# GpSimd takes up two of its transferred sums earlier, VectorE one sum one place earlier, and x and results are issued three slots later

## The chip, the cores and the metric

The kernel runs on one core of a Trainium2 chip. The metric is the device time of one execution in microseconds (us). Below, PE is TensorE, DVE is VectorE, ACT is ScalarE, POOL is GpSimd and SP is SyncE, as in the profile; a transfer is a DMA.

## The reference

The input is x, 8 sequences of 4096 tokens of 192 numbers. First comes a causal convolution over 7 tokens; its 7 weights come from a softmax and are shared by the 24 numbers of one of 8 heads. Then comes a two-layer network with an exact GELU between the products.

```
w = softmax(weight, axis=-1)                       # 8 heads x 7 taps
x_unf = x_pad[:, idx, :].reshape(B, S, K, H, 24)   # 6 zeros ahead of each sequence
x1 = einsum('hk,bskhg->bshg', w, x_unf)            # (8, 4096, 192)
h = x1.reshape(32768, 192) @ w_in                  # (192, 2048)
out = gelu(h) @ w_out                              # (2048, 192), float32
```

## The kernel before

**Tiles and stages.** The 32768 tokens are two halves of 16384; partitions 0 to 63 carry numbers of the first half and 64 to 127 of the second. A tile is 512 tokens of each half (the first six tiles have 256). For tile n, SP loads x in four transfers into one of three `xin` buffers (`load`, L570); DVE turns it so that the 192 numbers lie along the partitions (L747, letter `t` of `ORDER`) and computes the seven taps, two instructions for each tap (L775, letter `c`), into `xc`. In stage n, PE multiplies `xc` by `w_in` in 16 slots (`mm1`, L991); ACT applies the GELU to each slot's result (L896) and leaves `gT`. Between the slots of stage n, PE runs the second product of tile n-1. Its result is turned by DVE into `osb`, and SP stores that in four transfers (`store`, L590).

**The tiles with sums.** For tiles 6 to 33 the second product is written out by hand. Thirteen of them, the even tiles m = 8, 10, ..., 32 (`ST` in the code), use a scheme with fewer multiplications (`mm2_s`, L1129): it runs in stage m+1, and takes as operands four sums of blocks of `gT`, kept in `sst`. The sums are called S1, S3, Dn and S4. S1 and S3 are made in four pieces each (0 to 3), Dn and S4 in two. Dn adds to S1, and S4 adds to Dn. A piece of S1 or S3 needs the GELUs of four slots of stage m: piece 0 needs the first 3 or 4, piece 1 the first 7 or 8, piece 2 the first 11 or 12, piece 3 the first 15 or 16. The other tiles use the plain form (`mm2_t`, L1069).

**Who makes the sums.** Five pieces are made by transfers that POOL issues (`BY_DMA`): S3 pieces 0, 1, 2 and S1 pieces 0, 1. Each takes two transfers of 256 KB: a copy of the first operand from `gT` to `sst` (L494; POOL waits for the GELUs), and an adding transfer of the second operand (L497; POOL waits until the copy has landed). The other seven pieces are additions on DVE (L487, letters `1`, `3`, `d`, `4` of `ORDER` for S1, S3, Dn, S4). A piece 0 of Dn on DVE waits for the adding transfers of S1 pieces 0 and 1.

**Order on POOL.** The list `DMAS` gives each transfer a key; POOL's work is sorted by stage and key and then runs in that order, so a key is a place in a queue and no time. Besides, POOL copies the six tokens ahead of a tile (`halo`, L669) and issues three transfers after the second product of tile m (`st_move`): `p5s` (L504, 64 KB, in stage m+1 after ACT's copy L525 at its ninth slot), and `gsm` (L506) and `tq` (L509) in stage m+2.

**After the second product.** DVE combines the results in `st_post` (letter `p`): L538 waits for the `p5s` transfer, then a turn of x (L747) runs, then L541. PE's first plain multiplication of stage m+2 waits for L541.

**Order on DVE.** `ORDER` is a string written by hand: DVE runs one instruction for each letter, strictly in that order. `e` is an evacuation of results, `w` prepares weights.

**Order on SP.** Loads and stores go in pairs of stages. After tile m, SP waits until PE has finished a given slot of stage m+1 (semaphore `S_MM1`; `SL0[n]` is the number of slots before stage n) and then issues 16 transfers: the load of tile m+4, the store of tile m-2, the load of tile m+5 and the store of tile m-1, each as four transfers of 192 KB. The last two of these groups are shorter, 12 and 8 transfers.

## Time and profile before

| what | us |
|---|---|
| median of 3 runs | 673.85 (670.53 to 674.74) |
| the profiled execution | 671.07 |
| its span | 669.3 |
| stages 10, 12, ..., 34 (plain second product), each | 20.72 |
| stages 9, 11, 15, 21, 25, 29, 31 (after a tile with sums), each | 19.87 |
| stages 13, 17, 19, 23, 27, 33 (after a tile with sums) | 20.75, 20.00, 19.93, 20.00, 21.46, 20.60 |

A stage is counted from the end of the last `mm1` slot of the stage before to the end of its own last `mm1` slot, read from the ends of PE's instructions in the trace. The page's first part gives busy times, the fourth the chain of work that ended last, the fifth the costliest groups with the idle time of their engine just before them. The list of waits names who waited for whom, with the total, the number and the longest wait. A timeline lists the instructions of one engine: start, duration, engine, line, operation, tiles, count, and in brackets the idle time before. The trace also gives for each transfer the moment when its last part landed.

### The profile page before, as it was taken

How to read it: one execution, taken by the hardware profiler on the slowest of the kernel's cores; microseconds unless marked ns; L12 is line 12 of the kernel's file. 1: busy time of each engine (PE TensorE's matmuls, PEld its weight loads, DVE VectorE, ACT ScalarE, POOL GpSimd, SP SyncE). 2: the span in 40 equal slices, each digit the busy share in tenths (PEclk: the TensorE clock that was granted, in tenths of full speed). 3: DMA queues.
4: the chain of work that ended last, by engine and by line, in shares of the span. 5: the costliest groups of instructions: out<-in, count | busy, mean ns of one | idle time of the engine just before them, and what ended most of it. 6: DMA issues, size and time to landing. Idle time of an engine off the chain costs nothing.

```text
span 669.3 us, 27462 instructions
## 1 busy us (share of the span) xinstructions
PE 663.9 (99%) x12504; PEld 487.6 (73%) x12504; DVE 612.1 (91%) x704; ACT 594.3 (89%) x681; POOL 189.6 (28%) x230
## 2 busy tenths in 40 slices
PE   9999999999999999999999999999999999999998
PEld 8999655565655767678787777877767776777667
DVE  6999998889999999999999999999999999999621
ACT  8999988898998989989898998989979899898882
POOL 7000702315042250511505124150421504224000
PEclk9999999999999999999999999999999999999999
DMA  9435361967939479494886939569394693936333
GB/s 154 122 89 129 72 108 56 183 132 165 201 103 204 109 159 181 120 197 117 159 163 155 205 91 187 128 160 211 96 198 104 154 205 104 196 87 141 87 73 95
DMA packets 159075, 93.72 MB, mean 140 GB/s; under 512 B 129088, under 2 KB 152448, under 8 KB 158960
## 3 DMA queue, kind: packets, MB, share of 16 engines
q1 hardware_dynamic: 129136, 49.37, 35.5%
q0 software_dynamic: 28704, 42.02, 29.7%
q8 instruction: 98, 1.61, 1.0%
q10 hardware_dynamic: 1120, 0.59, 0.3%
q14 instruction: 17, 0.14, 0.1%
HBM read 28.31 MB, written 25.17 MB: 80 GB/s over the span
## 4 chain that ended last, share of the span: by engine, by line
PE 91%; DMA 4%; POOL 2%; issue 1%; ACT 1%; POOLq 0%
PE hp L991 46%; PE ob L1069 21%; PE ob L1129 17%; PE ob L1031 5%; DMA sst<-gT 4%; POOL sst L497 2%; PE ob L1185 1%; PE hp L1185 1%; PE hp L913 1%; POOL sst L494 1%; ACT gT L896 0%; PE ob L933 0%; PE ob L991 0%; ACT xc L243 0%; ACT osb L350 0%
## 5 line engine op out<-in xcount | busy, mean ns | idle before, releaser
L896 ACT ACTIVATE gT<-hp 128x1024 bf16<-128x1024 f32 x510 | 514.1, 1021 | 61.0 <-PE hp L991 54.7
L991 PE MATMUL hp<-xc,win 64*64 64x512 bf16 (+2 forms) x6036 | 440.1, 366 | 0.1
L775 DVE SCALAR_TENSOR_TENSOR acc<-xT,wcol,acc 128x1024 f32<-128x1024 f32 (+1 forms) x330 | 298.7, 972 | 4.6 <-ACT acc L864 3.9
L991 PEld LDWEIGHTS hp<-xc,win 64*64 64x64 bf16 (+1 forms) x6036 | 231.6, 106 | 90.9 <-ACT gT L896 7.8
L1069 PE MATMUL ob<-gT,wout 64*64 64x512 bf16 x2880 | 205.7, 376 | 0.0
L1129 PE MATMUL ob<-gT,wout 64*64 64x512 bf16 x1248 | 167.3, 376 | 0.0
L1069 PEld LDWEIGHTS ob<-gT,wout 64*64 64x64 bf16 x2880 | 113.2, 118 | 46.4
L1129 PE MATMUL ob<-sst,wst 64*64 64x512 bf16 x624 | 129.6, 376 | 2.1 <-DMA sst<-gT 2.1
L1129 PEld LDWEIGHTS ob<-gT,wout 64*64 64x64 bf16 x1248 | 83.6, 118 | 24.9
L497 POOL DMA_DIRECT2D sst<-gT x65 | 84.3, 1417 | 36.8 <-DMA sst<-gT 31.9
L747 DVE STREAM_TRANSPOSE xT<-xin 128x1536 f32<-128x1536 f32 (+2 forms) x39 | 74.7, 1925 | 1.6 <-DMA xin<-in_x_dram 1.4
L494 POOL DMA_DIRECT2D sst<-gT x65 | 52.2, 803 | 73.0 <-ACT gT L896 72.7
L775 DVE SCALAR_TENSOR_TENSOR xc<-xT,wcol,acc 128x1024 bf16<-128x1024 f32 (+1 forms) x66 | 61.6, 958 | 0.1
L487 DVE TENSOR_TENSOR sst<-gT,sst 128x2048 bf16<-128x2048 bf16 x52 | 61.4, 1231 | 0.1
L864 ACT ACTIVATE acc<-xT,wcol 128x512 f32<-128x512 f32 (+1 forms) x87 | 61.1, 702 | 0.0
L1129 PEld LDWEIGHTS ob<-sst,wst 64*64 64x64 bf16 x624 | 53.2, 107 | 7.7 <-DMA sst<-gT 3.5
L669 POOL COPY xT<-xT 128x18 f32<-128x18 f32 x30 | 28.0, 932 | 106.0 <-DVE xc L775 101.2
L1129 PE MATMUL ob<-gT,wst 64*64 64x512 bf16 x208 | 57.5, 376 | 0.0
L376 DVE STREAM_TRANSPOSE osb<-ob 128x512 f32<-128x512 f32 x45 | 40.6, 905 | 12.3 <-PE ob L1069 12.3
L1129 PE MATMUL ob<-sst,wout 64*64 64x256 bf16 x416 | 45.2, 269 | 0.0
L504 POOL DMA_DIRECT2D p5s<-p5s x13 | 7.4, 570 | 132.7 <-ACT p5s L525 132.7
L1031 PE MATMUL ob<-wout,gT 64*128 64x192 bf16 x768 | 41.9, 243 | 0.0
(74 smaller groups left out, 323.1 us busy)
## 6 DMA issues: line engine op xcount, KB each, us to landing
sst<-gT POOLq DMA_DIRECT2D x130, 256.0 KB, 3.9
out_dram<-osb SPq DMA_DIRECT2D x124, 192.0 KB, 4.6
xin<-in_x_dram SPq DMA_DIRECT2D x116, 192.0 KB, 4.8
tq<-uu POOLq DMA_DIRECT2D x13, 256.0 KB, 4.0
xin<-in_x_dram SPq DMA_DIRECT2D x18, 96.0 KB, 2.4
gsm<-uu POOLq DMA_DIRECT2D x13, 128.0 KB, 2.2
p5s<-p5s POOLq DMA_DIRECT2D x13, 64.0 KB, 4.8
wout<-in_moe_w_out_dram POOLq DMA_DIRECT2D x4, 192.0 KB, 4.5
```

The lines of the kernel that those rows point to most:

```text
L376: v.transpose(osb_t(m, j), bank(BK[m][j])).then_inc(S_EV)
L487: v.tensor_tensor(out, one, two, ALU.add).then_inc(S_SA[NS.index(name)])
L494: e.dma_start(out, one).then_inc(S_CP[name, q], 16)
L497: e.dma_start(out, two, accum_op=ALU.add).then_inc(S_AD[name, q], 16)
L747: v.transpose(out, src).then_inc(S_TR)
L775: ins = v.scalar_tensor_tensor(dst, src, wk, a, op0=ALU.mult, op1=ALU.add)
L864: a.activation(out=acc[n % 2][:, p * TB : p * TB + w], in_=ap(xT[n % 2], p * XW + HX, [[NP * XW, 128], [1, w]]), func=AF.Copy, scale=wcol[ ...
L896: a.activation(out=ap(gT[n % 2], i * c * 2 * w, dst), in_=ap(ob, 2 * TB, [[4 * TB, 128], *src[1:]]) if u < SL0[1] and u % 3 == 2 else ap(h ...
L991: ins = t.matmul(hbuf(u, slice(fo, fo + fw), o, w), ap(win, f1, [[NP * F, 64], [2, fw]]), xc[n % 2][r, p * TB : p * TB + w], start=(p == 0 ...
L1031: ins = t.matmul(bb[sub], gT[m % 2][r, c0 : c0 + 128], wout[r, CH[sub][i] * C : (CH[sub][i] + 1) * C], start=(ph == 0 and k == 0), stop=(p ...
L1069: ins = t.matmul(bank(BK[m][j], slice(64 * h, 64 * h + 64), w), ap(wout, 64 * hf * NF * C + CH[h][i] * C + j, [[NF * C, 64], [NP, 64]],), ...
L1129: ins = t.matmul(bank(BK[m][bk], slice(64 * cg, 64 * cg + 64), w), wt_, a[r, c0 : c0 + w], start=(e == mine[0]), stop=(e in (mine[-1], GRO ...
```

## The change

POOL's adding transfers of S3 piece 0 and S1 piece 0 (new keys 5.5 and 6.4) stand ahead of the copies of S3 piece 1 and S1 piece 1; before, both stood behind these copies and in the opposite order. So POOL's ten transfers of a tile, c for a copy and a for an adding one, were c S3.0, c S1.0, c S3.1, c S1.1, a S1.0, a S3.0, a S1.1, c S3.2, a S3.1, a S3.2 and are c S3.0, c S1.0, a S3.0, a S1.0, c S3.1, c S1.1, a S1.1, c S3.2, a S3.1, a S3.2. The other changed keys (9 to 9.6, 12 to 13) leave the order as it is; the last copy (S3.2, key 11) is ahead of the fourth sum (S3.1, key 11.1) in both.

On DVE, piece 0 of Dn moves ahead of one tap instruction: `1ccd3e1ed44` becomes `1cdc3e1ed44`, for tiles 10 to 30. For tile 8, `1ccde1ed344cc` becomes `1dc4e1ed34ccc`, and for tile 32, `1ccde1ed344` becomes `1cdce1ed344`.

SP's wait ahead of its 16 transfers is for slot 4 of stage m+1 where it was for slot 1.

```diff
-        DMAS = [(3, "S3", 0, 0), (4, "S1", 0, 0), (7, "S3", 1, 0), (8, "S1", 1, 0), (8.1, "S1", 0, 1), (8.2, "S3", 0, 1),
-                (9, "S1", 1, 1), (11, "S3", 2, 0), (11.1, "S3", 1, 1), (12, "S3", 2, 1)]
+        DMAS = [(3, "S3", 0, 0), (4, "S1", 0, 0), (5.5, "S3", 0, 1), (6.4, "S1", 0, 1), (7, "S3", 1, 0), (8, "S1", 1, 0),
+                (9.6, "S1", 1, 1), (11, "S3", 2, 0), (11.1, "S3", 1, 1), (13, "S3", 2, 1)]
...
         ORDER = (
...
-            "cccccccccetccccecccccccetcecc1ccde1ed344ccccccpctpcpeccccccccpccececet1ccd3e1ed44ccccccpcccptpcecccc"
+            "cccccccccetccccecccccccetcecc1dc4e1ed34cccccccpctpcpeccccccccpccececet1cdc3e1ed44ccccccpcccptpcecccc"
...
                 if at[0] - 1 in ST:
-                    sp.wait_ge(S_MM1, SL0[at[0]] + 1)
+                    sp.wait_ge(S_MM1, SL0[at[0]] + 4)
                 op(sp, n)
```

An entry of `DMAS` is (key, sum, piece, 0 for the copy or 1 for the adding transfer).

More of the change, by code (lines that the diff above doesn't have):

```diff
@@ L605, in bass_lightweight_conv__then__act_gelu_exact_kernel @@
             "tccccccccccccctccctccccccccccccwtcwcccccccccccwwwwctcccccccccccctcccccccccccccccccccccccccettceccccc"
-            "cccccccccetccccecccccccetcecc1ccde1ed344ccccccpctpcpeccccccccpccececet1ccd3e1ed44ccccccpcccptpcecccc"
-            "ccccpccececet1ccd3e1ed44ccccccpcccptpceccccccccpccececet1ccd3e1ed44ccccccpcccptpceccccccccpccececet1"
-            "ccd3e1ed44ccccccpcccptpceccccccccpccececet1ccd3e1ed44ccccccpcccptpceccccccccpccececet1ccd3e1ed44cccc"
-            "ccpcccptpceccccccccpccececet1ccd3e1ed44ccccccpcccptpceccccccccpccececet1ccd3e1ed44ccccccpcccptpceccc"
-            "cccccpccececet1ccd3e1ed44ccccccpcccptpceccccccccpccececet1ccd3e1ed44ccccccpcccptpceccccccccpccececet"
-            "1ccd3e1ed44ccccccpcccptpceccccccccpccecececc1ccde1ed344ccccccpcppepeeeeeeeee"
+            "cccccccccetccccecccccccetcecc1dc4e1ed34cccccccpctpcpeccccccccpccececet1cdc3e1ed44ccccccpcccptpcecccc"
+            "ccccpccececet1cdc3e1ed44ccccccpcccptpceccccccccpccececet1cdc3e1ed44ccccccpcccptpceccccccccpccececet1"
+            "cdc3e1ed44ccccccpcccptpceccccccccpccececet1cdc3e1ed44ccccccpcccptpceccccccccpccececet1cdc3e1ed44cccc"
+            "ccpcccptpceccccccccpccececet1cdc3e1ed44ccccccpcccptpceccccccccpccececet1cdc3e1ed44ccccccpcccptpceccc"
+            "cccccpccececet1cdc3e1ed44ccccccpcccptpceccccccccpccececet1cdc3e1ed44ccccccpcccptpceccccccccpccececet"
+            "1cdc3e1ed44ccccccpcccptpceccccccccpccecececc1cdce1ed344ccccccpcppepeeeeeeeee"
         )
```

## The prediction

> **What bounds the kernel.** I read the page's first part, then the list of waits, then the stages one by one, then the timelines around the stages that are too long.

> ```profile
> PE 663.9 (99%) x12504; PEld 487.6 (73%) x12504; DVE 612.1 (91%) x704; ACT 594.3 (89%) x681; POOL 189.6 (28%) x230
> ```
> ```profile
> DVE tq L538 <- DMA p5s<-p5s: 5.5, 8, 1.2
> ...
> PEld ob L1129 <- DMA sst<-gT: 3.5, 3, 1.7
> ...
> PE ob L1129 <- DMA sst<-gT: 2.1, 3, 1.2
> ```

> PE is busy 99% and the change leaves PE's program alone, so all that can be gained is the time in which PE stands. The plain stages all last 20.72 us: PE without a gap. The thirteen stages after a tile with sums last 19.87 when undisturbed; six are longer: stage 13 by 0.88, 17 by 0.13, 19 by 0.06, 23 by 0.13, 27 by 1.59 and 33 by 0.73, together 3.52. Without them the profiled execution would take 671.07 - 3.52 = 667.55. That is the floor, and it lies 0.9% under the median of 673.85. I count against 671.07; the median is 2.8 above it.

> The waits show three waits of PE for transferred sums. They are stages 13, 27 and 33 (3.20 of the 3.52). In all three it is S3 piece 2, the last one; stage 27, which begins at 491.14, shows how (POOL first, then SP's queue):

> ```profile
> 482.84 3.75 POOL L497 DMA_DIRECT2D sst<-gT  x3
> 486.25 1.09 POOL L494 DMA_DIRECT2D sst<-gT  x1
> 486.97 1.57 POOL L497 DMA_DIRECT2D sst<-gT  x1
> 492.75 1.18 POOL L497 DMA_DIRECT2D sst<-gT  x1 [4.21 <-issue]
> ```
> ```profile
> 492.25 1.92 SPq L570 DMA_DIRECT2D xin<-in_x_dram  x4
> ```

> The last adding transfer goes out at 492.75, after SP's loads of x began at 492.25, and lands at 498.76: 6.00 us. In stages 13 and 33 it goes out 0.3 after the loads and 0.3 before them, and takes 5.5 and 6.0. Of the ten quiet stages, seven lie between 4.1 and 4.5. Its copy, behind three adding transfers that occupy the engines from 482.8, had landed only at 491.75.

> The smaller excesses (17, 19, 23) are another wait: S1 piece 3, a DVE addition that PE needs early in the stage. I set its end against the stage's beginning: ends at 2.67, 2.75 and 2.93 us cost nothing, 3.00 costs 0.06, 3.06 and 3.07 cost 0.13. So from 2.94 on, each 0.1 us that DVE is late is 0.1 us of PE. What makes DVE late there is far ahead of it:

> ```profile
> 467.37 0.42 DVE L538 TENSOR_TENSOR tq<-ob,p5s 64x256 f32<-64x256 f32 x1 [1.09 <-DMA p5s<-p5s]
> 467.71 2.33 DVE L747 STREAM_TRANSPOSE xT<-xin 128x1536 f32<-128x1536 f32 x1
> ...
> 491.13 1.23 DVE L487 TENSOR_TENSOR sst<-gT,sst 128x2048 bf16<-128x2048 bf16 x1
> ...
> 493.63 0.66 DVE L487 TENSOR_TENSOR sst<-gT 128x1024 bf16<-128x1024 bf16 x1
> ```

> From L538, which waits for p5s, to the end of S1 piece 3 (494.29), DVE does not stop once: 26.92 us here, 26.87 to 27.08 in eleven of twelve pairs. A pair of stages is 20.72 + 19.87 = 40.59. So p5s may land until 2.94 + 40.59 - 26.95 - 0.09 = 16.49 us after the beginning of stage m+1 before PE pays. It lands at 16.23 to 16.75 in most pairs: this kernel stands exactly at that edge.

> **The change, part by part.** *POOL.* Nothing is added or removed: ten issues for each tile before and after. With times from the beginning of stage m, tile 20 has the copies of S3.0 and S1.0 landing at 8.43 and 9.18, then POOL idle to 10.42. a S3.0 now starts at 8.5 (its copy landed), a S1.0 behind it; two adding issues in a row end 2.5 after the first start (12.42 to 14.89 in the trace), so at 11.0. The copies c S3.1 and c S1.1, which now stand behind, started at 10.42 and 11.72 and took 0.71 each; they end at 11.7 and 12.4, as before. A lone adding transfer lands 3.67 after its issue, each further one 1.45 later: 12.2 and 13.6 for the two. The copies follow at about 0.65 each: c S1.1 at 14.9 (14.46 before). a S1.1 is issued then, and with no adding transfer in front of it lands at 14.95 + 3.67 = 18.6 (19.03 before). c S3.2 then lands at about 19.4 (20.25), and a S3.2 goes out at 19.5 and lands at 23.2 to 24.0 (24.99). PE needs it at 26.7. The next tile's halo copy (L669), behind a S3.2 in POOL's queue, moves up by 1 us with it and waits for nothing new.

> *SP.* Slot 4 ends 3.67 after slot 1 (25.47 against 21.80 from the beginning of stage m). So loads begin at 25.5, after the last sum has landed even if its copy is late by the 1.6 us of tile 12. Both moves take away the collision: **-3.20**. What hides the later loads: x lands 8.3 to 21.8 us before DVE turns it from tile 13 on to tile 33, 7.0 for tile 34, 5.8 for tile 12; less 3.67 leaves at least 2.1. The store of tile m-2 lands 11.9 into stage m+1, now about 15.6; the evacuation that needs its buffer comes at 21.2. The other store lands at 18.6, now 22.3, needed at 35. gsm and tq go out at 23.1, and DVE takes them 4.0 and 3.5 after they land. Without that cover each us of delay would be a us of DVE. So 0.

> *DVE.* Piece 0 of Dn moves ahead of one 1.2 us tap. It itself has 8.6 us to spare at PE, so nothing is gained; but DVE now asks for S1.1 about 0.6 after S1 piece 2 ends, at 18.6 to 19.5, and behind the waiting instruction stands S1 piece 3. For most tiles S1.1 at 18.1 to 19.2 is just in time. In tiles 10, 12 and 14 the first copy landed at 9.57 to 9.83, where tile 20 had 8.43; then POOL is held, c S1.1 ends at 13.6 to 13.8 and S1.1 lands at 19.7 to 20.0. DVE waits 0.95, 0.75 and 1.03; less the room of S1 piece 3 there (2.94 less its ends at 2.47, 2.96 and 2.67) PE stands 0.48, 0.77 and 0.76: **+2.0**. In tile 8 the earlier S4 piece 0 fills the same 3 us of DVE. Bounds: 0 if the copies are as in tile 28 (first landing 7.91), 13 x 0.8 = 10 if all are as tile 12.

> *p5s.* This transfer, issued 11.7 into stage m+1, stood in the last third of SP's 16 transfers (10.6 after their start) and now stands at 6.9. Across SP's backlog it lands as if it stood in one row with them: with 16 transfers it took 3.99 to 5.19, for tile 30 with 12 it took 3.77, for tile 32 with 8, all landed, 1.94.

> ```profile
> DMA to landing us min/median/max: 1.9/4.8/5.2
> ```

> From below: with nothing ahead of the loads, the first lands 2.4 after its issue (tile 32), at 7.2, and each next 0.89 later; ten or eleven are issued before p5s's descriptors are out at 12.3; p5s then lands at 15.5 or 16.4 and costs nothing. From above: SP's own transfers 6.9 us into the stream took up to 5.5; p5s took up to 0.85 more than SP's transfers of the same moment: 11.7 + 6.35 = 18.05, and (18.05 - 16.49) x 11 pairs = 17. I take eleven, 16.4, and so **0**, since the stream no longer starts with an interposed sum; the 0.32 of stages 17, 19 and 23 stays.

> [...]

> The sum: 671.07 - 3.20 + 2.0 + 0 = 669.9, rounded to **670.0**, 0.6% under the median, less than the 1% that a measurement of this kernel can tell from no change.

> **Rivals.** *p5s comes late* (slower). One more transfer ahead of it (twelve) is 0.89: 17.3, 11 x 0.8 = 9 us, 677. For: the loads no longer start behind a sum, so SP issues faster. It decides from a landing at 16.49 + 12/11 = 17.6 on: then 670 + 12 = 682, above the median by over 1%. Against: before, ten had been issued 7.5 us into the stream in most pairs. *DVE waits for S1.1 in every pair* instead of in three: 8 more than my +2.0, 678; for it speaks that the room is 0.3 to 0.7, against it the time of the copies in tiles 16 to 32. *The sum stays late*: it is the copies among themselves that delay S3.2, the stalls return, 671.1 to 674.

> **How the numbers follow.** My case, 667.5 to 672.5, gets 0.58; p5s late 0.17, of which 0.10 above 680 and 0.09 above 680.6 (1% over the median); DVE waiting everywhere 0.13, 672.5 to 681, 0.02 of it above 680 and 0.01 above 680.6; the sum still late 0.09; more than 1% faster (under 667.1, below the floor) 0.03. The range 667.2 to 680.0 leaves out the last, 0.10 of p5s late and 0.02 of DVE waiting: 0.15. Faster 0.03, same 0.87, slower 0.10.

> **What would show it.** No wait of PE or its weight loads for a DMA of sst. The last adding transfer landing 2.5 to 3.5 into stages 9, 11, ..., 33. All of these stages at 19.87 to 20.1, except 11, 13 and 15 at 20.3 to 20.7. A DVE wait for sst ahead of L487, absent now, in these three alone. p5s landing about 16.4 into its stage; if it lands at 17 or more, every second stage is longer by what is over 16.49, and the prediction is wrong on the slow side.

## The result, and the profile after

The changed kernel took 703.52 us (median of 4 runs, 699.19 to 705.77), the kernel before 672.62 on the same chip (4 runs, 670.53 to 674.74). The ratio is 1.045, with an interval of 1.039 to 1.052: slower by 30.9 us. The profiled execution took 703.16 us, its span is 701.4, which is 32.1 more than before.

The page of the changed kernel, its first part (busy time and share of each engine) and the first line of its fourth (the chain that ended last):

```profile
PE 675.1 (96%) x12504; PEld 496.6 (71%) x12504; DVE 612.8 (87%) x704; ACT 594.6 (85%) x681; POOL 190.2 (27%) x230
...
PE 30%; DMA 20%; ACT 12%; DVE 9%; issue 4%; POOL 4%; DVEq 0%; POOLq 0%
```

The numbers of instructions are the same as before, and PE has fallen from 99% to 96%. The chain no longer runs along PE (91% before): a fifth of it is transfers of sums. The list of waits says where PE stands now (total, times, longest, in us):

```profile
POOL sst L497 <- DMA sst<-gT: 108.5, 38, 4.7
...
DVE sst L487 <- DMA sst<-gT: 31.0, 13, 3.9
PEld ob L1129 <- DVE sst L487: 24.0, 12, 2.6
...
PE ob L1129 <- DVE sst L487: 18.3, 11, 2.1
...
PEld ob L1129 <- DVE tq L534: 8.0, 10, 1.4
```

DVE waits for a transferred sum in all 13 pairs of stages, where it waited in none before, and PE waits behind it, first for DVE's sums (L487) and then for L534, the first instruction of `st_post`. (The rows of PE and of its weight loads overlap and are not to be added.) POOL waits 108.5 us for its own copies. Before, it was:

```profile
POOL sst L497 <- DMA sst<-gT: 31.9, 17, 3.4
```

By stages: the plain ones still last 20.72 (one of them 20.80). Stages 9, 11, ..., 33 last 22.56, 24.51, 24.28, 22.98, 24.12, 23.20, 21.95, 21.62, 22.20, 22.58, 20.74, 21.96 and 20.50. Less 19.87 each that is an excess of 34.88, against 3.52 before: 31.4 of the 32.1 us. Stages 18 and 19 in the table of windows (stretch, its length, then for each engine the busy time and the number of instructions in the order PE, PEld, DVE, ACT, POOL, then granted clock, DMA share, GB/s):

```profile
326.68:347.40 20.72, 20.72 (x390) 14.86 (x384) 19.52 (x22) 18.68 (x21) 10.06 (x11) 1.00 0.48 113
347.40:370.61 23.21, 20.69 (x391) 13.96 (x385) 20.62 (x23) 18.53 (x22) 2.44 (x4) 1.00 0.85 172
```

PE is busy 20.72 of 20.72 in the plain stage and 20.69 of 23.21 in the next.

**One pair, tile 20.** Stage 20 begins at 370.61 and stage 21 at 391.33. POOL's timeline (start, duration, line, tiles, count; in brackets the idle time before and who ended it):

```profile
375.84 0.73 POOL L494 DMA_DIRECT2D sst<-gT  x1 [0.45 <-ACT gT L896]
376.93 0.72 POOL L494 DMA_DIRECT2D sst<-gT  x1 [0.36 <-ACT gT L896]
379.58 2.46 POOL L497 DMA_DIRECT2D sst<-gT  x2 [1.93 <-DMA sst<-gT]
381.05 2.49 POOL L494 DMA_DIRECT2D sst<-gT  x2
387.65 1.23 POOL L497 DMA_DIRECT2D sst<-gT  x1 [4.12 <-DMA sst<-gT]
```

The two adding transfers go out at 8.97 and 9.72 into the stage, and the copies c S3.1 and c S1.1 go out behind them at 10.45 and 12.20, within 0.5 of the time they had before. But then POOL waits 4.12 us: c S1.1 lands only at 16.76, and a S1.1 goes out at 17.05. DVE's timeline shows the other end of it:

```profile
388.59 0.64 DVE L487 TENSOR_TENSOR sst<-gT 128x1024 bf16<-128x1024 bf16 x1
389.16 0.73 DVE L775 SCALAR_TENSOR_TENSOR acc<-xT,wcol,acc 128x512 f32<-128x512 f32 x1
392.01 1.22 DVE L487 TENSOR_TENSOR sst<-gT,sst 128x2048 bf16<-128x2048 bf16 x1 [2.12 <-DMA sst<-gT]
393.15 1.28 DVE L775 SCALAR_TENSOR_TENSOR acc<-xT,wcol,acc 128x1024 f32<-128x1024 f32 x1
394.35 0.68 DVE L487 TENSOR_TENSOR sst<-gT 128x1024 bf16<-128x1024 bf16 x1
394.96 0.86 DVE L376 STREAM_TRANSPOSE osb<-ob 128x512 f32<-128x512 f32 x1
395.70 0.64 DVE L487 TENSOR_TENSOR sst<-gT 128x1024 bf16<-128x1024 bf16 x1
```

After S1 piece 2 and one tap instruction, DVE asks for S1.1 at 389.89. It has landed at 391.89; the piece of Dn starts at 392.01. The last line is S1 piece 3: it ends at 396.34, 5.01 into stage 21, and the prediction's limit for it was 2.94. That is 2.07 too late, and the stage is 2.08 too long.

### The profile page after: what moved, and what is told of

Its sections match the earlier page's. It is cut to its first block, busy times and chain, and to the rows that moved or that the text cites. A ratio compares the mean times of both kernels' runs of the same rounds, so it can differ in the third digit from the quotient of the medians.

```text
span 701.4 us, 27462 instructions
## 1 busy us (share of the span) xinstructions
PE 675.1 (96%) x12504; PEld 496.6 (71%) x12504; DVE 612.8 (87%) x704; ACT 594.6 (85%) x681; POOL 190.2 (27%) x230
## 4 chain that ended last, share of the span: by engine, by line
PE 30%; DMA 20%; ACT 12%; DVE 9%; issue 4%; POOL 4%; DVEq 0%; POOLq 0%
DMA sst<-gT 20%; PE hp L991 14%; PE ob L1129 11%; ACT gT L896 8%; DVE sst L487 4%; PE ob L1069 4%; POOL sst L497 3%; DVE acc L775 2%; ACT acc L864 2%; ACT uu L525 1%; DVE osb L376 1%; DVE tq L534 1%; PE ob L1185 1%; PE hp L1185 1%; DVE xc L775 0%
## 5 line engine op out<-in xcount | busy, mean ns | idle before, releaser
L991 PE MATMUL hp<-xc,win 64*64 64x512 bf16 (+2 forms) x6036 | 470.2, 368 | 0.9 <-DVE xc L775 0.8
L991 PEld LDWEIGHTS hp<-xc,win 64*64 64x64 bf16 (+1 forms) x6036 | 246.7, 106 | 89.1 <-ACT gT L896 7.4
L1069 PE MATMUL ob<-gT,wout 64*64 64x512 bf16 x2880 | 208.7, 376 | 0.0
L1129 PE MATMUL ob<-gT,wout 64*64 64x512 bf16 x1248 | 190.9, 383 | 0.0
L1129 PE MATMUL ob<-sst,wst 64*64 64x512 bf16 x624 | 134.8, 386 | 18.9 <-DVE sst L487 18.3
L1069 PEld LDWEIGHTS ob<-gT,wout 64*64 64x64 bf16 x2880 | 120.8, 118 | 39.2 <-issue 0.5
L497 POOL DMA_DIRECT2D sst<-gT x65 | 85.7, 1409 | 111.5 <-DMA sst<-gT 108.5
L1129 PEld LDWEIGHTS ob<-gT,wout 64*64 64x64 bf16 x1248 | 91.4, 119 | 15.1
L487 DVE TENSOR_TENSOR sst<-gT,sst 128x2048 bf16<-128x2048 bf16 x52 | 60.7, 1199 | 31.0 <-DMA sst<-gT 31.0
L1129 PEld LDWEIGHTS ob<-sst,wst 64*64 64x64 bf16 x624 | 53.1, 109 | 36.5 <-DVE sst L487 24.0
L747 DVE STREAM_TRANSPOSE xT<-xin 128x1536 f32<-128x1536 f32 (+2 forms) x39 | 74.7, 1925 | 2.7 <-DMA xin<-in_x_dram 2.5
L494 POOL DMA_DIRECT2D sst<-gT x65 | 64.2, 1101 | 21.8 <-ACT gT L896 21.6
L1129 PE MATMUL ob<-gT,wst 64*64 64x512 bf16 x208 | 57.6, 377 | 3.2 <-DVE tq L534 3.2
L669 POOL COPY xT<-xT 128x18 f32<-128x18 f32 x30 | 27.1, 904 | 111.5 <-DVE xc L775 105.7
L1129 PE MATMUL ob<-sst,wout 64*64 64x256 bf16 x416 | 46.8, 269 | 0.0
```

Source lines behind the costliest of these rows:

```text
L487: v.tensor_tensor(out, one, two, ALU.add).then_inc(S_SA[NS.index(name)])
L494: e.dma_start(out, one).then_inc(S_CP[name, q], 16)
L497: e.dma_start(out, two, accum_op=ALU.add).then_inc(S_AD[name, q], 16)
L747: v.transpose(out, src).then_inc(S_TR)
L991: ins = t.matmul(hbuf(u, slice(fo, fo + fw), o, w), ap(win, f1, [[NP * F, 64], [2, fw]]), xc[n % 2][r, p * TB : p * TB + w], start=(p == 0 ...
L1069: ins = t.matmul(bank(BK[m][j], slice(64 * h, 64 * h + 64), w), ap(wout, 64 * hf * NF * C + CH[h][i] * C + j, [[NF * C, 64], [NP, 64]],), ...
```

## The experiments

The change has three parts: POOL's order (`DMAS`), SP's slot and DVE's order (`ORDER`). In the short diffs below a change of `ORDER` is shown by the fragment that repeats for each pair. All ratios are against the kernel before, run beside it on the same chip. Three chips were used, and the kernel before had medians of 672.18, 675.52 and 674.96 us on them. Times of transfers are counted from the beginning of stage m; medians are over the 13 tiles. The trace has 16 landing records for each transfer; "first part" and "last part" are the moments of the first and the last of them. A wait is for all 16, as the kernel counts them (`then_inc(..., 16)`).

### One part at a time

**POOL's part alone.**

```diff
-        DMAS = [(3, "S3", 0, 0), (4, "S1", 0, 0), (7, "S3", 1, 0), (8, "S1", 1, 0), (8.1, "S1", 0, 1), (8.2, "S3", 0, 1),
-                (9, "S1", 1, 1), (11, "S3", 2, 0), (11.1, "S3", 1, 1), (12, "S3", 2, 1)]
+        DMAS = [(3, "S3", 0, 0), (4, "S1", 0, 0), (5.5, "S3", 0, 1), (6.4, "S1", 0, 1), (7, "S3", 1, 0), (8, "S1", 1, 0),
+                (9.6, "S1", 1, 1), (11, "S3", 2, 0), (11.1, "S3", 1, 1), (13, "S3", 2, 1)]
```

> Only GpSimd's order is changed; VectorE's string and SP's slot are those of before. In the changed kernel S1 piece 1 landed at 19.8 to 22.7 us into stage m, where it was at 19.0 to 20.6, and VectorE's piece 0 of Dn, at about 19.2, waited 0.6 to 3.9 us for it. Theory A (the lateness is made by GpSimd's order: S1.1 is late by 2 to 3 us, whoever asks for it): S1.1 lands at 21 to 22.6 here too; Dn asks at 20.4, one tap later, so it waits about 1.2 us less than in the changed kernel; with SP's loads again at slot 1, the last sum goes out at about 22 to 23.5, behind them. Time 685 to 695. Theory B (the three slots on SP make p5s late, and the Dn wait only follows): S1.1 lands at 19 and the time is 668 to 675.

Measured: 700.09 us (699.36 to 701.23), ratio 1.042 (1.039 to 1.045). S1.1 lands at 21.67, 19.08 before (medians). Its list of waits:

```profile
POOL sst L497 <- DMA sst<-gT: 109.4, 38, 4.7
...
PEld ob L1129 <- DMA sst<-gT: 23.6, 17, 3.0
...
PE ob L1129 <- DMA sst<-gT: 16.0, 15, 2.5
DVE sst L487 <- DMA sst<-gT: 14.8, 10, 2.5
PEld ob L1129 <- DVE sst L487: 11.3, 11, 1.4
```

POOL's new order alone brings a loss of nearly the same size, but not by the same path. Here PE waits for sums by DMA directly. Of these 23.6 us, 20.7 are for S3 piece 2 and 2.9 for S1 piece 1: a S3.2 goes out at 23.2, and SP's loads have begun before it at slot 1. It then takes 6.1 us and lands at 29.3. So the collision that the change was to remove became the rule. In the full change, with SP at slot 4, no such wait is for S3 piece 2.

**SP's part alone.**

```diff
-                    sp.wait_ge(S_MM1, SL0[at[0]] + 1)
+                    sp.wait_ge(S_MM1, SL0[at[0]] + 4)
```

> Only SP's 16 transfers are held to slot 4. Theory A: the collision of the last sum with the loads is gone, p5s lands 16.2 to 17 us into its stage; 667.5 to 672. Theory B: p5s lands at 17.5 or later and every second stage is longer by 1 us or more; 680 to 700.

Measured: 670.72 us (669.55 to 672.3, 10 runs), ratio 0.998 (0.9966 to 0.9995); the profiled execution took 670.35. Among PE's waits those for a DMA of sst are gone: a S3.2 takes 3.63 from issue to landing (4.53 before), and its latest landing is 26.04 (28.34 before). What is left is L534:

```profile
DVE tq L538 <- DMA p5s<-p5s: 6.1, 9, 1.6
...
PEld ob L1129 <- DVE tq L534: 2.2, 5, 0.6
```

p5s takes 4.1 to 5.4 us and lands at 15.8 to 17.1 into stage m+1 in twelve tiles (in tile 32 at 14.5). The five stages with an excess (0.46, 0.05, 0.51, 0.14 and 0.50) are exactly those in which L534 ends more than 13.34 into the stage, by the same amount: 13.80, 13.39, 13.85, 13.48 and 13.84. So SP's later slot does not make p5s late enough to bring the loss. In the full change p5s lands later still, at 18.2 (median), in stages that are themselves longer; but there DVE still has to wait for S1.1 in all 13 pairs, so a DVE that came earlier would only wait longer.

**DVE's part alone.**

```diff
-1ccd3e1ed44ccccccp
+1cdc3e1ed44ccccccp
```

> Only VectorE's string is changed. S1.1 lands at 19.0 to 20.6 as in the kernel before and Dn asks at 18.6 to 19.5. Theory A: VectorE waits 0 to 0.6 us in most stages; 671 to 678. Theory B: nothing, 670 to 674.

Measured: 674.07 us (671.77 to 677.74), ratio 1.004 (1.002 to 1.006), not to be told from no change at the 1% that the prediction went by. S1.1 lands at 19.00 to 20.10, as before, and DVE waits for it seven times, 2.8 us in all:

```profile
DVE sst L487 <- DMA sst<-gT: 2.8, 7, 0.8
```

**POOL's and SP's parts together** (both diffs above).

> GpSimd's order and SP's slot are changed, VectorE's string is that of before. Theory A: S1.1 lands at 21 to 22.6, Dn asks at 20.4 and waits 0.5 to 2 us; the excess of the changed kernel falls by about 1.2 us for each of 12 pairs: 684 to 692. Theory B: as the changed kernel, 700 to 705.

Measured: 683.37 us (682.66 to 687.73), ratio 1.018 (1.014 to 1.022). S1.1 is as late as in the full change (21.33; 21.55 there), but DVE's waits are short:

```profile
PEld ob L1129 <- DVE sst L487: 8.9, 10, 1.4
DVE sst L487 <- DMA sst<-gT: 8.6, 8, 1.5
PEld ob L1129 <- DVE tq L534: 8.1, 12, 0.7
```

The same late transfer costs an excess of 14.91 us here and 34.88 with the new `ORDER`. The move of Dn takes one 1.2 us tap out of the time before DVE asks, and with it the cover: by estimate 13 x 1.2 = 15.6 of the difference of 20.0. Another 3.4 are a slower clock (below). So the parts do not add: DVE's costs 0.4% alone, and takes 1.8% to 4.5% on top of the other two.

### Why S1.1 is late

In the changed kernel the copy c S1.1 goes out at the old time (11.89 against 11.73) and lands at 17.05 instead of 14.70. Two accounts were left: the bytes of the two adding transfers that now stand ahead of the copies, or POOL itself, held by issues and waits.

**One sum ahead instead of two** (only a S3.0; slot 4; `ORDER` of before; the diff is against the changed kernel).

```diff
-        DMAS = [(3, "S3", 0, 0), (4, "S1", 0, 0), (5.5, "S3", 0, 1), (6.4, "S1", 0, 1), (7, "S3", 1, 0), (8, "S1", 1, 0),
-                (9.6, "S1", 1, 1), (11, "S3", 2, 0), (11.1, "S3", 1, 1), (13, "S3", 2, 1)]
+        DMAS = [(3, "S3", 0, 0), (4, "S1", 0, 0), (5.5, "S3", 0, 1), (7, "S3", 1, 0), (8, "S1", 1, 0), (8.1, "S1", 0, 1),
+                (9.6, "S1", 1, 1), (11, "S3", 2, 0), (11.1, "S3", 1, 1), (13, "S3", 2, 1)]
```

> As the run with GpSimd's order and SP's slot changed and VectorE's string as before (683.4 us), but only one adding transfer, S3 piece 0, stands ahead of the copies of S3.1 and S1.1; that of S1.0 stays behind them. Theory A1 (the copies stand in one row behind the bytes of the adding transfers, and S1.1 waits for its copy): each adding transfer taken out of the row gives back 1.4 to 2.3 us; S1.1 lands at 19 to 20.5 instead of 20.8 to 22.8 and the time is 669 to 675. Theory A2 (GpSimd is held at its first wait for a copy, and all that is behind it is late): the hold is the same; S1.1 at 20.8 to 22.8, 680 to 686.

Measured: 678.61 us (676.36 to 682.6), ratio 1.004 (1.001 to 1.007). The time lies between what the two accounts expect, and decides nothing. c S1.1 lands at 16.05, between 14.70 and 17.05; but a S1.0 then stands ahead of a S1.1, and S1.1 is no earlier (21.56). (These landings are of the slowest of the ten runs, 682.6 us.)

**The two sums ahead made short** (both new places, slot 4, `ORDER` of before; the adding transfers of S3.0 and S1.0 move an eighth of their columns, so seven eighths of these two additions are left out).

```diff
+                if q == 0:
+                    cut = [[NF * 2 * TB, 128], [4 * TB, 2], [1, TB // 8]]
+                    two = ap(two.tensor, two.offset, cut)
+                    out = ap(out.tensor, out.offset, [[NF // 2 * TB, 128], [TB, 2], [1, TB // 8]])
                 e.dma_start(out, two, accum_op=ALU.add).then_inc(S_AD[name, q], 16)
```

> GpSimd's order and SP's slot as in the changed kernel, VectorE's string as before; the adding transfers of S3.0 and S1.0 move only an eighth of the columns, in as many pieces, so that seven eighths of these two additions are left out. The order, the waits and the number of issues stay. Theory A1 (bytes ahead of the copies): the copy of S1.1 lands at 14.2 to 15.6, S1.1 at 18.0 to 19.6; 668 to 673. Theory A2 (GpSimd held, or its issues being slow): the copy still lands at 16 to 18 and the time is 680 to 686.

Measured: 671.33 us (670.43 to 672.3), ratio 0.994 (0.991 to 0.997). POOL does the same as with the full sums: it issues at 9.08, 9.82, 10.56 and 11.74 (8.94, 9.69, 10.46 and 11.72 in the run of POOL's and SP's parts). But c S1.1 lands at 15.35 instead of 16.85, and S1.1 at 19.73 instead of 21.33. The excess falls from 14.91 to 3.24. POOL's timeline of tile 20 (stage 20 begins at 349.28; lines are four higher, L501 is the adding issue):

```profile
358.33 2.46 POOL L501 DMA_DIRECT2D sst<-gT  x2 [2.01 <-DMA sst<-gT]
359.81 2.47 POOL L494 DMA_DIRECT2D sst<-gT  x2
364.35 1.23 POOL L501 DMA_DIRECT2D sst<-gT  x1 [2.07 <-DMA sst<-gT]
```

The wait ahead of a S1.1 is 2.07 where the changed kernel has 4.12, behind issues of the same length (2.46 and 2.47). So it is not POOL's issues: of the 2.15 us by which c S1.1 is late with the full sums (16.85 against 14.70), 1.50 go with seven eighths of the two transfers' bytes. The other 0.65 stay, and no run takes them apart.

### How a late S1.1 becomes time of PE

Dn piece 0 was moved behind S1 piece 3, first with SP's part alone and then with POOL's and SP's.

```diff
-1ccd3e1ed44ccccccp
+1cc3e1ded44ccccccp
```

> GpSimd as before, SP at slot 4, and piece 0 of Dn is asked for behind S1 piece 3 instead of ahead of it (1cc3e1ded44). Dn.0 has 8 to 9 us to spare at PE, S1.3 has 0 to 0.8. If PE's last excess in the run with SP's slot alone (1.7 us in stages 13, 15, 17, 31, 33) comes from S1.3 being late by p5s and by what stands ahead of it on VectorE, S1.3 comes 1 us earlier and nearly all second stages take 19.87: 667.5 to 669.5. If it does not, 670 to 672.

Measured: 672.78 us (671.85 to 674.84), ratio 0.997 (0.994 to 0.999). S1 piece 3 is ready 1.1 to 1.4 us before PE needs it, and yet every one of the 13 stages is longer by 0.22 to 0.70, with one wait:

```profile
PEld ob L1129 <- DVE tq L534: 5.5, 13, 0.8
```

So the small excesses in stages 17, 19 and 23 of the kernel before were not S1 piece 3, as the prediction had it and as this run expected. They are L534, on the same unbroken stretch of DVE's work, and the list of waits of the kernel before says so:

```profile
PEld ob L1129 <- DVE tq L534: 0.6, 3, 0.2
```

> GpSimd's order and SP's slot as in the changed kernel, with piece 0 of Dn asked for behind S1 piece 3. S1.1 lands as late as before this move, 20.8 to 22.8. Theory A (what costs is S1.3 standing behind a waiting Dn, not S1.1 itself): S1.3 is on time, Dn asks at 22.5 and waits little; PE asks for S1.1 itself at 22.0 to 22.4, so some stages lose up to 0.9 us: 669 to 676. If the lateness of S1.1 costs in itself, 680 to 686 as without the move.

Measured: 676.44 us (674.21 to 682.26), ratio 1.002 (0.999 to 1.005), while S1.1 is as late as ever (21.83). With S1 piece 3 out of the way of the wait, the excess is 9.29 instead of 14.91. It is now PE that waits for sums by DMA:

```profile
PEld ob L1129 <- DMA sst<-gT: 8.2, 10, 2.2
```

Of these 8.2 us, 5.3 are for S3 piece 2, which stands behind a S1.1 in POOL's queue, and 2.8 (in five stages) for S1 piece 1. So part of the cost of a late S1.1 is what stands behind Dn on DVE, part is the last sum behind it on POOL, and the smallest part is S1.1 itself.

### A version that gains

Two kernels with SP's part alone: one with L534 (`p`) a tap earlier, and one unchanged, for comparison on the same chip.

```diff
-ed44ccccccpc
+ed44cccccpcc
```

> GpSimd as before, SP at slot 4, Dn where it was, and VectorE's first combination of a tile with sums (L534) one tap earlier (44cccccpcc for 44ccccccpc). In the run with SP's slot alone PE's weight loads waited for L534 in five stages, 2.2 us in all, and L534 ended 13.1 to 13.9 us into the stage; a stage lost time where it ended after about 13.34. If that is what was left, L534 ends at 12.3 to 12.8, no stage waits for it, and the excess falls from 1.7 to 0 to 0.6 us: 1 to 1.7 us under the run with SP's slot alone. If S1 piece 3 is what was left (as the prediction had it), the excess stays.

> SP's slot alone once more, beside the run with the earlier combination on the same chip: 0.2 to 0.5% faster than the kernel before.

Measured: 669.10 us (668.45 to 669.65), ratio 0.992 (0.989 to 0.995), with the earlier L534; 669.53 (668.73 to 671.15), ratio 0.993 (0.990 to 0.996), without. In the first PE no longer waits for L534 at all; but in this execution of the second that wait was only 0.6 us, so the two can't be told apart. Both ratios are below 1, but neither reaches the 1% that the prediction asked of a measured difference. SP's part alone gave 668.7 to 672.3 in 17 runs on two chips, while the kernel before gave 669.8 to 676.9 on the same two in 31 of 32 runs (681.0 in the other). That fits a last sum that meets SP's loads in some executions and not in others; it was shown in single traces, not run by run.

## Why the prediction was wrong

The forecast was 670.0 in a range to 680.0; 703.5 came.

**The step that failed** is in POOL's part: "A lone adding transfer lands 3.67 after its issue, each further one 1.45 later: 12.2 and 13.6 for the two. The copies follow at about 0.65 each: c S1.1 at 14.9 ... a S1.1 is issued then, and ... lands at 14.95 + 3.67 = 18.6". In tile 20 the first four issues came as predicted to 0.5 us. What the transfers did (tile 20, us into the stage):

| transfer | predicted landing | first part | last part |
|---|---|---|---|
| a S3.0 | 12.2 | 12.48 | 14.74 |
| a S1.0 | 13.6 | 13.88 | 15.48 |
| c S1.1 | 14.9 | 15.14 | 16.76 |
| a S1.1 | 18.6 | 20.53 | 21.28 |

The first parts of the first three agree with the working to 0.3 us. The last parts are 1.6 to 2.3 later, and a wait ends with the last. So the term that was mis-sized is the landing of c S1.1: 16.76 where the working had 14.9, and a S1.1 went out at 17.05 instead of 14.95. In the kernel before the two moments lay close together where the prediction took its prices: the spread from first to last part was 0.20 for a S1.0, 0.24 for c S3.1 and 0.72 for c S1.1 (medians). In the changed kernel it is 1.55, 1.56 and 1.59, and the lag is passed on to a S1.1. The rows that I priced by showed adding transfers behind copies, and I used them for copies behind adding transfers. The two moments are far apart there: 12.48 and 14.74 in the table belong to one transfer.

How the last part lags can be read from the traces, if the tiles are taken one by one. It is mostly one part of the 16: in eleven of the 13 tiles the first 15 parts of c S1.1 landed within 0.26 us, and the last one 0.51 to 2.10 us after the first. What falls together with it in time is an instruction load, a packet of 16 KB that took 0.88 to 2.03 us in the changed kernel. That a load holds up one part is my reading; the trace does not name the engine of either. The page of the changed kernel counts the loads (packets, MB, share):

```profile
q8 instruction: 98, 1.61, 1.0%
```

The clearest case is c S3.0, which goes out with no other copy or sum of its tile ahead of it. There are 156 of these in the twelve kernels. With an instruction load while it was under way (120 of them) its spread was 0.73 to 2.24; without one (36) it was 0.17 to 0.35. (In the 26 of the kernel before and the changed one: 0.75 to 2.17 with a load, 20 of them, and 0.17 to 0.35 without.) The kernel before shows the same at c S3.1: 0.96 to 1.48 in the six tiles in which a load began 11.2 to 11.6 into the stage, and 0.20 to 0.24 in the other seven, in which it began earlier or later. The median of 0.24 hides this. What is new in the changed kernel is that the lag lasts. Before, the first part of a S1.0 landed 1.96 after that of c S1.1, and the lag was gone by then (0.72, then 0.20). In the changed kernel the first parts of the four follow each other at 1.39, 0.68 and 0.63, and the lag stays to the end of the row. A load began 11.0 to 14.0 into the stage there, among these transfers, in all tiles but 32; in that tile it began at 10.0, and the spread of c S1.1 was the smallest, 0.51 (0.70 to 2.10 elsewhere). With the short sums ahead it was 0.19 (median). No run moved a load: this is an agreement in time, without an exception at c S3.0, and not an experiment.

**From the landing on, the working holds.** In tile 20 S1 piece 3 ends 4.45 after S1.1 has landed, and must end by 2.94 into stage m+1; so S1.1 may land until 20.72 + 2.94 - 4.45 = 19.2. It lands at 21.55 (median): 2.35 late, times 13 is 30.6 of the excess of 34.88.

**The rival "DVE waits for S1.1 in every pair"** is what happened. It was given 0.13, and its price was too low: 0.8 us for each pair, worked out from tile 12 with a landing at 20.0 as the worst case. The measured landings go up to 22.65, past every one that the prediction had. The bound used the same price for a transfer's end, so it fell with it. (The other rival's price, 677 with p5s late, is added up without the +2.0 of the forecast; with it, it is 679, and still within the range.) The nearest row for the other end was in the trace: a S3.1, behind another transfer in the same queue, had a spread of 1.67 in the kernel before.

**A term that was missing:** PE's clock. In stages 11, 13 and 17 the excess is 1.14 more than what L534 is late by; in the other ten it is equal to that within 0.01. (L534 is late by what it ends after 13.34 into the stage.) These three alone have a granted clock of 0.93 in the windows. 3 x 1.14 = 3.4 us.

**What was right.** SP's part does what was claimed: with it alone no wait of PE for a sum is left, and the later loads and stores cost nothing. In that run p5s took 4.1 to 5.4 in SP's stream, as the rows said, and landed at 15.8 to 17.1 but for the last tile (predicted 16.4, bounds 15.5 and 18.05). The limit at 16.49 came out nearly right although its reason was wrong: it was put to S1 piece 3, and the wait is for L534, 10.4 us later on the same unbroken chain of DVE. The last sum was predicted to go out at 19.5, and before SP's loads at 25.5; it goes out at 23.3 and lands at 26.9 (25.2 before), so what SP gained was used up by POOL's delay. PE does not wait for it, but five times, 2.8 us in all, for S1 piece 1.

## What to carry to other kernels

Price a transfer by its last part, take that price from a place where the same kinds stand in the same order, and look at it tile by tile, since a median can hide every second case: a copy behind two adding transfers landed 2.4 us later than a copy issued 0.2 us earlier without them. Before an instruction that waits is moved forward on an engine that runs in strict order, ask how late the awaited thing may be before the instructions behind it are late; the 1.2 us tap that was taken out of the way turned 1.8% into 4.5%. When three edits are made at once, run each alone: here POOL's cost 4.2%, and each of the other two stayed within 1%. Then look where each one's waits are: POOL's part alone lost most of its time at another sum than the full change did.

## What the runs showed of the hardware that was not expected

```profile
172.49:175.90 3.41, 1.32 (x28) 0.62 (x24) 3.41 (x6) 1.19 (x2) 0.59 (x2) 1.00 0.48 77
175.90:179.31 3.41, 3.41 (x40) 1.76 (x36) 3.41 (x4) 1.25 (x2) 0.00 (x0) 0.50 0.29 75
261.23:264.64 3.41, 1.65 (x32) 0.77 (x24) 3.41 (x5) 2.05 (x2) 1.65 (x2) 1.00 0.58 92
264.64:268.05 3.41, 3.09 (x60) 2.02 (x64) 3.41 (x5) 1.49 (x2) 0.00 (x0) 1.00 0.22 52
```

PE runs 40 matmuls in the second window and 60 in the fourth, although it is busy 3.41 us in the second and 3.09 in the fourth: busy time alone does not show this, the granted clock does. The matmul lasts 0.63 us in the one and 0.38 in the other; PE's timeline of stage 17, the first instruction after the stall and one of those after it:

```profile
308.60 0.40 PE L1129 MATMUL ob<-sst,wst 64*64 64x512 bf16 x1 [2.09 <-DVE sst L487]
...
310.35 0.63 PE L1129 MATMUL ob<-sst,wst 64*64 64x512 bf16 x1
```

With POOL's part alone the same is seen once, in stage 9 after a wait of 2.5 (0.93 over the stage).

What differs between the three and the two is where the stall falls. The three stretches of half clock begin at 175.90, 220.28 and 309.02, which are 44.38 and 88.74 apart: 13 and 26 times 3.413. So in this trace the clock changed in steps of 3.41 us. In stages 11, 13 and 17 the whole stall lies in one such interval (172.89 to 174.97 in the first window above), and the next interval has half clock. In stages 15 and 19 a boundary, counted on in the same steps, cuts the stall: 262.88 to 264.96 at 264.64, 351.64 to 353.73 at 353.40. At most 1.77 us of it lie in one interval, and the clock stays. In this trace and in that of the kernel before, no interval with 1.77 us of idle time or less was followed by a half clock during the work. So PE had stood for 2.09 us of the 3.41 ahead of each of these half clocks, and for 1.77 at most where the clock stayed. These are five stalls, and no run moved one across a boundary: what sets the clock is not shown.
